# Partial sums of a seven-product block matmul: added up in one PSUM bank and copied by ScalarE, or added on VectorE

## The chip, the core and the metric

The kernel runs on one core of one Trainium2 chip. The metric is the device time of one execution in microseconds. The kernel before takes 2735.14 us (median of three runs, 2733.68 to 2735.2). A core has TensorE (PE in the profile), which multiplies matrices into the eight banks of PSUM; ScalarE (ACT) and VectorE (DVE), which read PSUM and work elementwise; GpSimd (POOL); and DMA queues, most of them issued by SyncE (SP). Each engine has its own list of instructions, and semaphores order the engines against each other.

## What is computed

Eight images of 3008 tokens and 256 channels in float32 go through a filter in the frequency domain, and then through a two-layer network with ELU between the layers:

```
X = rfft(x, axis=1);  y = irfft(X * (filt_r + 1j*filt_i), n=3008, axis=1)
x = y.reshape(8 * 3008, 256)
h = x @ w_in                                   # 256 -> 2048
g = where(h > 0, h, exp(min(h, 0)) - 1)        # ELU
return g @ w_out                               # 2048 -> 256
```

## The kernel before

The transforms are done by matmuls with small tables (units `a_unit`, `b_unit`, `bi_unit`, `n_unit`). The two layers are done in **items**: one item is one image `b` (8), one block `m` of 512 tokens (6 per image; block 0 has 448) and one quarter `q` (4) of the 2048 hidden channels, 192 items in all. Both layers see their matrices as 2 by 2 blocks and use seven block products in place of eight; sums of blocks are made before and after. An item has seven products of the first layer ("up", U1 to U7) and, one item later, seven of the second ("down", D1 to D7). Every product is two matmuls of 128 by 128 by 256 in float32, which the profile shows as four MATMUL records.

The products of the first layer go to banks of the pool `psM`, four banks used in turn; the second layer's sums stay in four banks `po0` to `po3` over the four quarters.

```python
    psM = pool("psM", 4, space=PSUM)
...
        def mm(n, key, start):                 # product n of the first layer into bank `key`
            if start:
                banks[key] = psM.tile([P, 2, 256], FP32, tag="mx", name="ph" + key)
            for a in range(2):
                nc.tensor.matmul(banks[key][:, a, 0:h], w_in[q][:, COMBO[n], a, :], y[n],
                                 start=start and a == 0, stop=True, skip_group_check=True)   # L310
            return banks[key][:, :, 0:h]
        def add(o, i0, i1):                                                                  # L315
            nc.vector.tensor_tensor(out=g[o], in0=i0, in1=i1, op=ALU.add)
        def elu_exp(n, src):                   # exp(-relu(-h)), two operations on ScalarE
            e = es[n] = ep.tile([P, 2, 256], FP32, tag="e", name="e")[:, :, 0:h]
            nc.scalar.activation(out=e, in_=src, func=AXT.Relu, scale=-1.0)                  # L321
            nc.scalar.activation(out=e, in_=e, func=AXT.Exp, scale=-1.0)                     # L322
        def elu_max(n, src):                   # max(e - 1, h) on VectorE
            nc.vector.scalar_tensor_tensor(out=g[n], in0=es[n], scalar=1.0, in1=src, ...)    # L326

        def s1(): nc.scalar.activation(out=g["t1"], in_=mm(1, "a", True), func=AXT.Copy)     # L330
        def s6(): add("t2", mm(6, "b", True), g["t1"])
        def s2(): p = mm(2, "a", False); elu_exp("b11", p); elu_max("b11", p)
        def s5(): add("t4", mm(5, "c", True), g["t2"])
        def s7(): add("b22", mm(7, "d", True), g["t4"]); elu_exp("b22", g["b22"])
        def s3(): add("b12", mm(3, "c", False), g["t2"]); elu_max("b22", g["b22"])
        def s4(): elu_exp("b12", g["b12"]); add("b21", mm(4, "d", False), g["t2"])
        def tail():
            elu_exp("b21", g["b21"]); elu_max("b12", g["b12"])
            # t1 = b12 - b11; b12 = b22 - b12; elu_max b21; t2 = b22 - t1; t4 = b21 - t2    (L359 to L363)
```

(The one-line bodies are printed here in place of several lines each.) The tail's four subtractions make the block sums that the second layer's products take. In the last quarter, q = 3, the second layer's four banks are put together into the output block `c`, on VectorE after the item's own tail:

```python
        def step(n):                           # product n of the second layer
            ...matmuls into po...                                                            # L383
            if q == 3 and n in (5, 7):
                t = k[i] = kp.tile([P, 2, 256], FP32, tag="k%d" % i, name="k%d" % i)
                nc.scalar.activation(out=t[:, :, 0:h], in_=po[i][:, :, 0:h], func=AXT.Copy)  # L387
                if n == 7:
                    p3 = t[:, 0, 0:h]
                    nc.vector.tensor_tensor(out=p3, in0=p3, in1=k[0][:, 1, 0:h], op=ALU.add) # L390
        def tail():                            # q == 3 alone: six adds of 128x256
            add(c12, po[2][:, 1, 0:h], p1); add(c11, po[2][:, 0, 0:h], p1); add(p7, p7, c12) # L401
            add(c12, c12, p35); add(c21, po[3][:, 0, 0:h], p7); add(c22, p7, p5)
```

The main loop writes the steps of item `i` and of item `i-1` in a fixed order, with units of the transforms at two places, in the middle and at the end:

```python
            for k in "UDUDUDUUD":              # U1 D1 U6 D3 U2 D5 U5 U7 D7
                ...
            for fn, a in plan.get((i, 0), ()): # a_unit, n_unit, o_unit (output transposes)
                fn(*a)
            for k in "UDUDD":                  # U3 D6 U4 D2 D4
                ...
            up_tail(); down_tail()
            for fn, a in plan.get((i, 1), ()): # bi_unit, b_unit, n_unit
                fn(*a)
```

The units at the places repeat with every image, that is, every 24 items. By the place of an item in its image: `a_unit` in the middle of items 0, 2, 3, 4, 6, 7; `o_unit`, two transposes on VectorE, in the middle of items 1, 5, 9, 13, 17, 21; `n_unit` in the middle of items 8, 12, 16, 20 and at the end of 1 and 5; `b_unit` at the end of items 9 to 16 and `bi_unit` at the end of 11 to 18. A `b_unit` has four multiplications of 128x512 on VectorE that read its two banks.

Of the kernel before, what the change touches and what calls it, by code (L numbers as in the profile page):

```python
# [10 lines left out]
FP32 = mybir.dt.float32  # L11
U32 = mybir.dt.uint32
AXT = mybir.ActivationFunctionType
# [82 lines left out]
def kernel(  # L96
# [15 lines left out]
    def pool(name, bufs, **kw):  # L112
        return ctx.enter_context(tc.tile_pool(name=name, bufs=bufs, **kw))
# [13 lines left out]
    yd = pool("yd", 2, space=DRAM)  # L127
    fdp = pool("fdp", 1, space=DRAM)
    psO = pool("psO", 1, space=PSUM)
    psM = pool("psM", 4, space=PSUM)  # L130

    gb, gr, gi = (glob.tile([P, 2, 64], FP32, name=n) for n in ("gb", "gr", "gi"))

# [7 lines left out]

    def raw(src, row, ap, col=0):
        return bass.AP(tensor=src.tensor, offset=src.offset + row * D + col, ap=ap)

# [12 lines left out]
    def a_unit(b, c):  # L159
        t = t1s[b, c] = t1p.tile([P, XC, D], FP32, tag="t1", name="t1")  # L160
        xt, w = xs.pop((b, c)), tas.pop((b, c))
        for r in (0, 2):
            ps = psM.tile([P, 2, D], FP32, tag="mx", name="psa")
            for u in range(2):
                nc.tensor.matmul(ps[:, u, :], w[:, r + u, :], xt[:, r + u, :], start=True, stop=True)  # L165
            nc.scalar.activation(out=t[:, r:r + 2, :], in_=ps, func=AXT.Copy)

# [41 lines left out]
    def b_unit(b, g, f=None):  # L211
        t = t2s.pop((b, g))
        f = fbufs[(b * NG + g) % FBUFS] if f is None else f
        re, im = (psM.tile([P, 2, D], FP32, tag="mx", name=n) for n in ("psr", "psi"))
        for o, a in ((0, 0), (64, 2)):
            for ps, k in ((re, LO), (im, HI)):
                tile_mm(ps[o:o + 64], gb, k, t[:, a:a + 2, :], g == 0 and a == 0)
        sr, si = (sp.tile([P, 2, D], FP32, tag=n, name=n) for n in ("sr", "si"))
        p, q = (qp.tile([P, 2, D], FP32, tag=n, name=n) for n in ("sp", "sq"))

        nc.vector.tensor_tensor(out=sr, in0=re, in1=f[:, 0], op=ALU.mult)
        nc.vector.tensor_tensor(out=si, in0=re, in1=f[:, 1], op=ALU.mult)  # L222
        nc.vector.tensor_tensor(out=p, in0=im, in1=f[:, 1], op=ALU.mult)  # L223
        nc.vector.tensor_tensor(out=q, in0=im, in1=f[:, 0], op=ALU.mult)
        nc.gpsimd.tensor_tensor(out=sr, in0=sr, in1=p, op=ALU.subtract)  # L225
        nc.gpsimd.tensor_tensor(out=si, in0=si, in1=q, op=ALU.add)
        ss[b, g] = (sr, si)

    def bi_unit(b, g):
        s = ss.pop((b, g))  # L230
        t = t3s[b, g] = t3p.tile([P, 4, D], FP32, tag="t3", name="t3")
        pa, pb = (psM.tile([P, 2, D], FP32, tag="mx", name=n) for n in ("pva", "pvb"))
        for o, table, sv in ((0, gr, s[0]), (64, gi, s[1])):
            for ps, k in ((pa, LO), (pb, HI)):
                tile_mm(ps[o:o + 64], table, k, sv, g == 0 and k == LO)
        nc.scalar.activation(out=t[:, 0:2, :], in_=pa, func=AXT.Copy)  # L236
        nc.scalar.activation(out=t[:, 2:4, :], in_=pb, func=AXT.Copy)

    def y_write(b, g):
        if g == 0:  # L240
# [16 lines left out]
    def n_unit(b, m):  # L257
        t, w, h = t4s.pop((b, m)), tns.pop((b, m)), half(m)
        rows = []
        for dh in range(2):  # L260
            y = yp.tile([P, 512], FP32, tag="y%d" % dh, name="y%d" % dh)
            ps = psM.tile([P, 512], FP32, tag="mx", name="psn")
            for q, i in enumerate(order(m)):
                nc.tensor.matmul(ps[:, ts(q, P)], t[:, i - 4 * m, ds(dh * P, P)], w[:, i - 4 * m, :],  # L264
                                 start=True, stop=True)
            nc.scalar.activation(out=y[:, 0:2 * h], in_=ps[:, 0:2 * h], func=AXT.Copy)
            rows += [y[:, 0:h], y[:, h:2 * h]]
        s = yp.tile([P, 3, 256], FP32, tag="ys", name="ys")
        ys[b, m] = combine(*rows, *(s[:, i, 0:h] for i in range(3)))
# [20 lines left out]
        return {1: b11, 2: b21, 3: b22, 4: t4, 5: t1, 6: t2, 7: b12}  # L290

    G_TAGS = (("g1", ("b11", "b12")), ("g2", ("b21", "b22")), ("g3", ("t1", "t2")), ("g4", ("t4",)))
    UPS = (1, 6, 2, 5, 7, 3, 4)
    DOWNS = (1, 3, 5, 7, 6, 2, 4)

    def up_steps(b, m, q):

        h = half(m)
        y = ys[b, m]
        g = {}  # L300
        for tag, names in G_TAGS:
            t = gp.tile([P, len(names), 2, 256], FP32, tag=tag, name=tag)
            g.update({n: t[:, i, :, 0:h] for i, n in enumerate(names)})
        banks = {}

        def mm(n, key, start):
            if start:
                banks[key] = psM.tile([P, 2, 256], FP32, tag="mx", name="ph" + key)
            for a in range(2):
                nc.tensor.matmul(banks[key][:, a, 0:h], w_in[q][:, COMBO[n], a, :], y[n],  # L310
                                 start=start and a == 0, stop=True, skip_group_check=True)
            return banks[key][:, :, 0:h]

        def add(o, i0, i1):
            nc.vector.tensor_tensor(out=g[o], in0=i0, in1=i1, op=ALU.add)  # L315

        es = {}

        def elu_exp(n, src):
# [4 lines that stand above are left out]
        def elu_max(n, src):  # L324

            nc.vector.scalar_tensor_tensor(out=g[n], in0=es[n], scalar=1.0, in1=src, op0=ALU.subtract, op1=ALU.max)  # L326


        def s1():
            nc.scalar.activation(out=g["t1"], in_=mm(1, "a", True), func=AXT.Copy)  # L330

        def s6():
            add("t2", mm(6, "b", True), g["t1"])

        def s2():
            p = mm(2, "a", False)
            elu_exp("b11", p)
            elu_max("b11", p)

        def s5():  # L340
            add("t4", mm(5, "c", True), g["t2"])

        def s7():
            add("b22", mm(7, "d", True), g["t4"])
            elu_exp("b22", g["b22"])

        def s3():
            add("b12", mm(3, "c", False), g["t2"])
            elu_max("b22", g["b22"])

        def s4():
            elu_exp("b12", g["b12"])
            add("b21", mm(4, "d", False), g["t2"])

        def tail():
            elu_exp("b21", g["b21"])
            elu_max("b12", g["b12"])
            t1, b12, b22 = g["t1"], g["b12"], g["b22"]
            nc.vector.tensor_tensor(out=t1, in0=b12, in1=g["b11"], op=ALU.subtract)  # L359
            nc.vector.tensor_tensor(out=b12, in0=b22, in1=b12, op=ALU.subtract)  # L360
            elu_max("b21", g["b21"])
            nc.vector.tensor_tensor(out=g["t2"], in0=b22, in1=t1, op=ALU.subtract)
            nc.vector.tensor_tensor(out=g["t4"], in0=g["b21"], in1=g["t2"], op=ALU.subtract)  # L363
            g_of[b, m, q] = {1: g["b11"], 2: g["b21"], 3: b22, 4: g["t4"], 5: t1, 6: g["t2"], 7: b12}

        return (s1, s6, s2, s5, s7, s3, s4), tail


    PLACE = {1: (0, 0), 5: (0, 1), 3: (1, 0), 7: (1, 1), 2: (2, 0), 6: (2, 1), 4: (3, 0)}

    def down_steps(b, m, q):
# [7 lines left out]
        def step(n):  # L379
            i, u = PLACE[n]  # L380
            for a in range(2):

                nc.tensor.matmul(po[i][:, u, 0:h], w_out[q][:, COMBO[n], a, :], g[n][:, a, :],  # L383
                                 start=q == 0 and a == 0 and n in (1, 3, 6, 4), stop=True, skip_group_check=True)
            if q == 3 and n in (5, 7):
                t = k[i] = kp.tile([P, 2, 256], FP32, tag="k%d" % i, name="k%d" % i)
                nc.scalar.activation(out=t[:, :, 0:h], in_=po[i][:, :, 0:h], func=AXT.Copy)  # L387
                if n == 7:
                    p3 = t[:, 0, 0:h]
                    nc.vector.tensor_tensor(out=p3, in0=p3, in1=k[0][:, 1, 0:h], op=ALU.add)  # L390

        def tail():
            if q != 3:
# [6 lines left out]
            def add(o, i0, i1):  # L400
                nc.vector.tensor_tensor(out=o, in0=i0, in1=i1, op=ALU.add)  # L401

            add(c12, po[2][:, 1, 0:h], p1)
            add(c11, po[2][:, 0, 0:h], p1)
            add(p7, p7, c12)
# [110 lines left out]
    with tc.manual_schedule():  # L516
# [109 lines left out]
        for i in range(-PER, len(items) + 2):  # L626
            ups, up_tail = up_steps(*items[i]) if 0 <= i < len(items) else ((), None)
            downs, down_tail = down_steps(*items[i - 1]) if 1 <= i <= len(items) else ((), None)
            ups, downs = list(ups), list(downs)
            for k in "UDUDUDUUD":  # L630
                s = ups if k == "U" else downs
                if s:
                    s.pop(0)()
            for fn, a in plan.get((i, 0), ()):
                fn(*a)
            for k in "UDUDD":
                s = ups if k == "U" else downs
                if s:
                    s.pop(0)()
# [38 lines left out]
```

## Time and profile before

| | before |
|---|---|
| time, median of three | 2735.14 us |
| span of the profiled run | 2733.4 us |
| MATMUL records of the two layers (L310, L383) | 10752 |
| granted TensorE clock, mean | 0.978 |
| HBM traffic | 79 GB/s over the span |
| down products (L383), busy | 1325.1 us |
| ScalarE relu and exp (L321, L322), busy | 948.0 us |
| VectorE adds on products (L315), busy | 647.3 us |

The profile gives each engine's busy time, and groups of instructions by source line and tile. Matmuls are pipelined and their ends are modelled, so two MATMUL records on one engine overlap; the distance from one start to the next says more than the duration. The granted clock is that of TensorE; it was at half for several stretches of the first 219 us and for the last 11 us, and full between.

### The profile page before, as it was taken

Reading aid. Unit: us, or ns where it says so; the run is one execution under the profiler, and the core shown is the slowest. Engines: PE = TensorE matmul, PEld = TensorE weight load, DVE = VectorE, ACT = ScalarE, POOL = GpSimd, SP = SyncE. Lnnn points to the kernel's source line nnn. Section 1 sums busy time; section 2 is a strip of 40 time slices with the busy share of each in tenths; the row PEclk is TensorE's granted clock in tenths of the full one; section 3 lists DMA queues with packets and bytes.
Section 4 is the critical chain, followed back from the end, with each engine's and each line's share of the span. In section 5 each row is a group of like instructions: output and inputs, shape, how many; then the busy total and the mean of one; then the engine's idle time right before and its main releaser. Section 6 shows DMA issues by size and latency. Waiting matters only on the chain.

```text
span 2733.4 us, 36388 instructions
## 1 busy us (share of the span) xinstructions
PE 2626.5 (96%) x12992; PEld 2237.5 (82%) x12992; DVE 2066.9 (76%) x3531; ACT 1286.0 (47%) x2177; POOL 275.6 (10%) x325
## 2 busy tenths in 40 slices
PE   2689999999999999999999999999999999999998
PEld 1278778987899878998789877898789987898887
DVE  3877877778777777768876787777877777777876
ACT  2244454544545444454444445454454544444443
POOL 4311210002000120001200021000210012000000
PEclk7599999999999999999999999999999999999999
DMA  9645321434114331242323333143421323110100
GB/s 244 180 116 122 88 69 37 110 96 102 43 42 121 78 93 37 74 120 68 79 50 88 88 85 73 37 110 97 98 57 41 79 62 95 37 39 19 26 22 16
DMA packets 229428, 214.47 MB, mean 78 GB/s; under 512 B 131620, under 2 KB 192566, under 8 KB 229248
## 3 DMA queue, kind: packets, MB, share of 16 engines
q1 hardware_dynamic: 210592, 173.65, 25.8%
q0 software_dynamic: 17792, 36.93, 5.6%
q8 instruction: 103, 1.69, 0.3%
q10 hardware_dynamic: 864, 1.57, 0.2%
q14 instruction: 77, 0.63, 0.1%
HBM read 136.97 MB, written 78.12 MB: 79 GB/s over the span
## 4 chain that ended last, share of the span: by engine, by line
PE 77%; DVE 12%; ACT 5%; DMA 2%; issue 2%; POOL 0%; DVEq 0%; SPq 0%; ACTq 0%; POOLq 0%
PE po L383 34%; PE pha L310 11%; PE phc L310 10%; PE phd L310 10%; PE phb L310 5%; DVE g L315 3%; PE psa L165 3%; ACT e L322 2%; ACT e L321 2%; PE pva L209 2%; PE psn L264 2%; PE psr L209 2%; DVE c L401 2%; DVE g L326 1%; DVE g L359 1%
## 5 line engine op out<-in xcount | busy, mean ns | idle before, releaser
L383 PE MATMUL po<-g,wo 128*128 128x256 f32 (+1 forms) x5376 | 1325.1, 375 | 0.0
L383 PEld LDWEIGHTS po<-g,wo 128*128 128x128 f32 x5376 | 1022.0, 190 | 116.4
L321 ACT ACTIVATE e<-g 128x512 f32<-128x512 f32 (+1 forms) x576 | 357.6, 621 | 616.2 <-DVE g L315 616.2
L322 ACT ACTIVATE e<-e 128x512 f32<-128x512 f32 (+1 forms) x768 | 477.5, 622 | 24.3
L310 PE MATMUL pha<-y,wi 128*128 128x256 f32 (+1 forms) x1536 | 396.2, 380 | 9.3 <-ACT g L330 9.2
L326 DVE SCALAR_TENSOR_TENSOR g<-e,g 128x512 f32<-128x512 f32 (+1 forms) x576 | 387.0, 672 | 12.9 <-ACT e L322 12.8
L315 DVE TENSOR_TENSOR g<-phc,g 128x512 f32<-128x512 f32 (+1 forms) x384 | 257.7, 671 | 141.3 <-PE phc L310 141.3
L321 ACT ACTIVATE e<-pha 128x512 f32<-128x512 f32 (+1 forms) x192 | 112.9, 588 | 532.5 <-PE pha L310 532.5
L310 PEld LDWEIGHTS pha<-y,wi 128*128 128x128 f32 x1536 | 285.3, 190 | 93.3 <-ACT t L236 34.1
L326 DVE SCALAR_TENSOR_TENSOR g<-e,pha 128x512 f32<-128x512 f32 (+1 forms) x192 | 129.4, 674 | 253.8 <-ACT e L322 253.8
L315 DVE TENSOR_TENSOR g<-phd,g 128x512 f32<-128x512 f32 (+1 forms) x384 | 260.6, 679 | 70.1 <-PE phd L310 50.0
L225 POOL TENSOR_TENSOR sr<-sr,sp 128x512 f32<-128x512 f32 x64 | 81.0, 1265 | 1289.4 <-DVE sp L223 1289.4
L310 PE MATMUL phc<-y,wi 128*128 128x256 f32 (+1 forms) x768 | 196.3, 378 | 5.0 <-DVE g L315 5.0
L310 PE MATMUL phc<-ys,wi 128*128 128x256 f32 (+1 forms) x768 | 195.3, 377 | 2.6 <-DVE si L222 2.6
L310 PE MATMUL phd<-y,wi 128*128 128x256 f32 (+1 forms) x768 | 194.7, 376 | 1.3
L310 PE MATMUL phd<-ys,wi 128*128 128x256 f32 (+1 forms) x768 | 194.2, 375 | 0.0
L310 PE MATMUL phb<-ys,wi 128*128 128x256 f32 (+1 forms) x768 | 193.8, 375 | 0.4 <-DVE ys L288 0.4
L310 PEld LDWEIGHTS phc<-y,wi 128*128 128x128 f32 x768 | 140.6, 190 | 29.5 <-DVE g L315 13.3
L310 PEld LDWEIGHTS phc<-ys,wi 128*128 128x128 f32 x768 | 145.3, 191 | 23.7 <-issue 7.8
L310 PEld LDWEIGHTS phd<-y,wi 128*128 128x128 f32 x768 | 144.7, 190 | 22.4 <-PE phc L310 6.5
L330 ACT ACTIVATE g<-pha 128x512 f32<-128x512 f32 (+1 forms) x192 | 112.7, 587 | 103.9 <-PE pha L310 103.7
L310 PEld LDWEIGHTS phd<-ys,wi 128*128 128x128 f32 x768 | 146.4, 191 | 16.7
(105 smaller groups left out, 2706.3 us busy)
## 6 DMA issues: line engine op xcount, KB each, us to landing
z<-t SPq DMA_DIRECT2D x192, 128.0 KB, 4.1
t<-z SPq DMA_DIRECT2D x128, 192.0 KB, 3.7
yd<-t SPq DMA_DIRECT2D x128, 192.0 KB, 2.8
t<-yd SPq DMA_DIRECT2D x192, 128.0 KB, 3.9
xc<-in_x_dram SPq DMA_DIRECT2D x84, 256.0 KB, 4.7
f<-fd POOLq DMA_DIRECT2D x112, 192.0 KB, 3.8
out_dram<-o SPq DMA_DIRECT2D x640, 32.0 KB, 1.6
tn<-tn_t SPq DMA_DIRECT2D x48, 256.0 KB, 3.8
```

The lines of the kernel that those rows point to most:

```text
L165: nc.tensor.matmul(ps[:, u, :], w[:, r + u, :], xt[:, r + u, :], start=True, stop=True)
L209: nc.tensor.matmul(ps[:, u:u + w, :], table[k, v, :], rhs[k, u:u + w, :], start=True, stop=True)
L225: nc.gpsimd.tensor_tensor(out=sr, in0=sr, in1=p, op=ALU.subtract)
L264: nc.tensor.matmul(ps[:, ts(q, P)], t[:, i - 4 * m, ds(dh * P, P)], w[:, i - 4 * m, :], start=True, stop=True)
L310: nc.tensor.matmul(banks[key][:, a, 0:h], w_in[q][:, COMBO[n], a, :], y[n], start=start and a == 0, stop=True, skip_group_check=True)
L315: nc.vector.tensor_tensor(out=g[o], in0=i0, in1=i1, op=ALU.add)
L321: nc.scalar.activation(out=e, in_=src, func=AXT.Relu, scale=-1.0)
L322: nc.scalar.activation(out=e, in_=e, func=AXT.Exp, scale=-1.0)
L326: nc.vector.scalar_tensor_tensor(out=g[n], in0=es[n], scalar=1.0, in1=src, op0=ALU.subtract, op1=ALU.max)
L330: nc.scalar.activation(out=g["t1"], in_=mm(1, "a", True), func=AXT.Copy)
L383: nc.tensor.matmul(po[i][:, u, 0:h], w_out[q][:, COMBO[n], a, :], g[n][:, a, :], start=q == 0 and a == 0 and n in (1, 3, 6, 4), stop=True, ...
L401: nc.vector.tensor_tensor(out=o, in0=i0, in1=i1, op=ALU.add)
```

## The change

In the first layer, products 1, 6, 5 and 3 now add up one after the other in one PSUM bank, "s". After each of the first three ScalarE copies the sum so far to SBUF (t1, t2, t4); after the fourth, b12 is read from the bank itself. Before, t2, t4 and b12 were made by adds on VectorE, and b11 was left in PSUM; now b11 is made by an add on VectorE. So per item two VectorE adds become ScalarE copies. The purpose is to take work from VectorE. Banks are now handed out by a list in the program, since "s" is held from U1 to U3 while others come and go. The order of the steps is changed to go with this. In the second layer's last quarter the two copies of `po0` and `po1` stand together after D7, and the add of L390 moves into the tail, which has seven adds instead of six. The number of matmuls is the same.

```diff
-    psM = pool("psM", 4, space=PSUM)
+    psM = pool("psM", 1, space=PSUM)
...
+    banks = [0, 1, 2, 3]
+    def bank(name, shape=(P, 2, D)):
+        i = banks.pop(0)
+        return i, psM.tile(list(shape), FP32, tag="m%d" % i, name=name)
...  (a_unit, b_unit, bi_unit, n_unit: take a bank from the list, give it back after the last reader)
-    UPS = (1, 6, 2, 5, 7, 3, 4)
+    UPS = (1, 2, 6, 5, 7, 3, 4)
...
         def s1():
-            nc.scalar.activation(out=g["t1"], in_=mm(1, "a", True), func=AXT.Copy)
+            keep("t1", mm(1, "s", True))
+        def s2():
+            add("b11", mm(2, "a", True), g["t1"])
+            done("a")
         def s6():
-            add("t2", mm(6, "b", True), g["t1"])
-        def s2():
-            p = mm(2, "a", False)
-            elu_exp("b11", p)
-            elu_max("b11", p)
+            keep("t2", mm(6, "s", False))
+            elu_exp("b11", g["b11"])
+            elu_max("b11", g["b11"])
         def s5():
-            add("t4", mm(5, "c", True), g["t2"])
+            keep("t4", mm(5, "s", False))
         def s7():
             add("b22", mm(7, "d", True), g["t4"])
-            elu_exp("b22", g["b22"])
         def s3():
-            add("b12", mm(3, "c", False), g["t2"])
+            p = mm(3, "s", False)
+            elu_exp("b12", p)
+            elu_exp("b22", g["b22"])
+            elu_max("b12", p)
+            done("s")
+        def s4():
+            add("b21", mm(4, "d", False), g["t2"])
+            done("d")
             elu_max("b22", g["b22"])
-        def s4():
-            elu_exp("b12", g["b12"])
-            add("b21", mm(4, "d", False), g["t2"])
         def tail():
             elu_exp("b21", g["b21"])
-            elu_max("b12", g["b12"])
...
-            if q == 3 and n in (5, 7):      (copy of one bank after D5, of the other after D7, add of L390)
+            if q == 3 and n == 7:
+                for i in range(2):
+                    t = k[i] = kp.tile([P, 2, 256], FP32, tag="k%d" % i, name="k%d" % i)
+                    nc.scalar.activation(out=t[:, :, 0:h], in_=po[i][:, :, 0:h], func=AXT.Copy)
...
+            add(p35, p35, p5)               (first of the tail's adds)
...
-            for k in "UDUDUDUUD":           (U1 D1 U6 D3 U2 D5 U5 U7 D7, units, U3 D6 U4 D2 D4)
+            for k in "UUDUDDU":             (U1 U2 D1 U6 D3 D5 U5, units, D7 U7 U3 D6 U4 D2 D4)
...
-            for k in "UDUDD":
+            for k in "DUUDUDD":
```

(`keep` is a ScalarE copy to SBUF; `done` puts a bank back on the list.)

More of the change, by code (lines that the diff above doesn't have):

```diff
@@ L162, in a_unit @@
         for r in (0, 2):
-            ps = psM.tile([P, 2, D], FP32, tag="mx", name="psa")
+            k, ps = bank("psa")
             for u in range(2):
@@ L166, in a_unit @@
             nc.scalar.activation(out=t[:, r:r + 2, :], in_=ps, func=AXT.Copy)
+            banks.append(k)
     def z_write(b, c):
@@ L213, in b_unit @@
         f = fbufs[(b * NG + g) % FBUFS] if f is None else f
-        re, im = (psM.tile([P, 2, D], FP32, tag="mx", name=n) for n in ("psr", "psi"))
+        (i0, re), (i1, im) = (bank(n) for n in ("psr", "psi"))
         for o, a in ((0, 0), (64, 2)):
@@ L224, in b_unit @@
         nc.vector.tensor_tensor(out=q, in0=im, in1=f[:, 0], op=ALU.mult)
+        banks.extend((i0, i1))
         nc.gpsimd.tensor_tensor(out=sr, in0=sr, in1=p, op=ALU.subtract)
@@ L231, in bi_unit @@
         t = t3s[b, g] = t3p.tile([P, 4, D], FP32, tag="t3", name="t3")
-        pa, pb = (psM.tile([P, 2, D], FP32, tag="mx", name=n) for n in ("pva", "pvb"))
+        (i0, pa), (i1, pb) = (bank(n) for n in ("pva", "pvb"))
         for o, table, sv in ((0, gr, s[0]), (64, gi, s[1])):
@@ L237, in bi_unit @@
         nc.scalar.activation(out=t[:, 2:4, :], in_=pb, func=AXT.Copy)
+        banks.extend((i0, i1))
     def y_write(b, g):
@@ L261, in n_unit @@
             y = yp.tile([P, 512], FP32, tag="y%d" % dh, name="y%d" % dh)
-            ps = psM.tile([P, 512], FP32, tag="mx", name="psn")
+            k, ps = bank("psn", (P, 512))
             for q, i in enumerate(order(m)):
@@ L266, in n_unit @@
             nc.scalar.activation(out=y[:, 0:2 * h], in_=ps[:, 0:2 * h], func=AXT.Copy)
+            banks.append(k)
             rows += [y[:, 0:h], y[:, h:2 * h]]
@@ L303, in up_steps, with done, keep @@
             g.update({n: t[:, i, :, 0:h] for i, n in enumerate(names)})
-        banks = {}
+        held = {}
         def mm(n, key, start):
             if start:
-                banks[key] = psM.tile([P, 2, 256], FP32, tag="mx", name="ph" + key)
+                held[key] = bank("ph" + key)
+            ps = held[key][1]
             for a in range(2):
-                nc.tensor.matmul(banks[key][:, a, 0:h], w_in[q][:, COMBO[n], a, :], y[n],
+                nc.tensor.matmul(ps[:, a, 0:h], w_in[q][:, COMBO[n], a, :], y[n],
                                  start=start and a == 0, stop=True, skip_group_check=True)
-            return banks[key][:, :, 0:h]
+            return ps[:, :, 0:h]
+        def done(key):
+            banks.append(held.pop(key)[0])
         def add(o, i0, i1):
             nc.vector.tensor_tensor(out=g[o], in0=i0, in1=i1, op=ALU.add)
+        def keep(o, i0):
+            nc.scalar.activation(out=g[o], in_=i0, func=AXT.Copy)
         es = {}
@@ L329, in s1, with s3 @@
         def s1():
-            nc.scalar.activation(out=g["t1"], in_=mm(1, "a", True), func=AXT.Copy)
+            keep("t1", mm(1, "s", True))
+        def s2():
+            add("b11", mm(2, "a", True), g["t1"])
+            done("a")
         def s6():
-            add("t2", mm(6, "b", True), g["t1"])
-        def s2():
-            p = mm(2, "a", False)
-            elu_exp("b11", p)
-            elu_max("b11", p)
+            keep("t2", mm(6, "s", False))
+            elu_exp("b11", g["b11"])
+            elu_max("b11", g["b11"])
         def s5():
-            add("t4", mm(5, "c", True), g["t2"])
+            keep("t4", mm(5, "s", False))
         def s7():
             add("b22", mm(7, "d", True), g["t4"])
+        def s3():
+            p = mm(3, "s", False)
+            elu_exp("b12", p)
             elu_exp("b22", g["b22"])
-        def s3():
-            add("b12", mm(3, "c", False), g["t2"])
+            elu_max("b12", p)
[3 more added lines that the diff above has]
+            done("d")
             elu_max("b22", g["b22"])
-        def s4():
-            elu_exp("b12", g["b12"])
-            add("b21", mm(4, "d", False), g["t2"])
         def tail():
             elu_exp("b21", g["b21"])
-            elu_max("b12", g["b12"])
             t1, b12, b22 = g["t1"], g["b12"], g["b22"]
@@ L364, in tail @@
             g_of[b, m, q] = {1: g["b11"], 2: g["b21"], 3: b22, 4: g["t4"], 5: t1, 6: g["t2"], 7: b12}
-        return (s1, s6, s2, s5, s7, s3, s4), tail
+        return (s1, s2, s6, s5, s7, s3, s4), tail
     PLACE = {1: (0, 0), 5: (0, 1), 3: (1, 0), 7: (1, 1), 2: (2, 0), 6: (2, 1), 4: (3, 0)}
@@ L384, in step @@
                                  start=q == 0 and a == 0 and n in (1, 3, 6, 4), stop=True, skip_group_check=True)
[L385 to L390, printed above, removed]
+            if q == 3 and n == 7:
+                for i in range(2):
+                    t = k[i] = kp.tile([P, 2, 256], FP32, tag="k%d" % i, name="k%d" % i)
+                    nc.scalar.activation(out=t[:, :, 0:h], in_=po[i][:, :, 0:h], func=AXT.Copy)
         def tail():
@@ L401, in add @@
                 nc.vector.tensor_tensor(out=o, in0=i0, in1=i1, op=ALU.add)
+            add(p35, p35, p5)
             add(c12, po[2][:, 1, 0:h], p1)
@@ L629 @@
             ups, downs = list(ups), list(downs)
-            for k in "UDUDUDUUD":
+            for k in "UUDUDDU":
                 s = ups if k == "U" else downs
```

## The prediction, made before the changed kernel ran

> **What bounds the kernel now.** First the page's busy times, then the table of a few windows, then the timeline of one item. The page:
>
> ```profile
> PE 2626.5 (96%) x12992; PEld 2237.5 (82%) x12992; DVE 2066.9 (76%) x3531; ACT 1286.0 (47%) x2177; POOL 275.6 (10%) x325
> ```
>
> PE at 96% could still hide small waits, so I looked at windows: a plain item (only the 14 products), then two items behind a q = 3 item, one without a unit at its end and one with (us, busy us and count of PE, PEld, DVE, ACT, POOL).
>
> ```profile
> 446.31:458.40 12.09, 12.09 (x57) 10.64 (x56) 8.80 (x15) 5.74 (x10) 0.00 (x0) 1.00 0.42 100
> 1238.50:1252.16 13.66, 13.48 (x70) 10.88 (x68) 13.13 (x24) 6.60 (x12) 0.00 (x0) 1.00 0.08 15
> 1295.60:1310.50 14.90, 14.62 (x76) 10.80 (x72) 14.50 (x27) 6.58 (x12) 3.50 (x4) 1.00 0.38 94
> ```
>
> In the plain item TensorE is full: 14 products in 12.09 us, one start each 0.863 us, no gap. There DVE (8.80) has room. Behind a q = 3 item DVE is nearly full too (13.13 of 13.66, 14.50 of 14.90). The timeline of the second window shows what that does, DVE first, then PE (start, us, what; idle before and who ended it):
>
> ```profile
> 1241.94 0.69 DVE L363 TENSOR_TENSOR g<-g,g 128x512 f32<-128x512 f32 x1
> 1242.55 0.75 DVE L401 TENSOR_TENSOR c<-po,k 128x256 f32<-128x256 f32 x2
> ...
> 1244.35 0.42 DVE L401 TENSOR_TENSOR c<-k,k 128x256 f32<-128x256 f32 x1
> 1244.68 0.68 DVE L315 TENSOR_TENSOR g<-phb,g 128x512 f32<-128x512 f32 x1
> 1245.28 0.68 DVE L326 SCALAR_TENSOR_TENSOR g<-e,pha 128x512 f32<-128x512 f32 x1
> 1245.87 0.68 DVE L315 TENSOR_TENSOR g<-phc,g 128x512 f32<-128x512 f32 x1
> ```
>
> ```profile
> 1245.41 1.03 PE L383 MATMUL po<-g,wo 128*128 128x256 f32 x4
> 1246.61 1.13 PE L310 MATMUL phc<-y,wi 128*128 128x256 f32 x4 [0.17 <-DVE g L315]
> ```
>
> The previous item's last subtraction starts 3.44 us after this item began (1238.50), then come the six adds of `c` (2.13 us), and only at 6.18 us the first add of this item. U3 accumulates into bank phc, which the add at 1245.87 to 1246.55 still reads; so U3 starts at 1246.61, 8.11 us in, not at 9 x 0.863 = 7.77. **The wait is 0.34 us**, and its products then take 0.967 instead of 0.863 us to the next, since their first weight load lies bare.
>
> Going through all PE starts of the trace, after 250 us only places 9, 13, 17 and 21 of an image's 24 items have such waits: about 0.35, 0.70, 0.70 and 0.15 us, 1.9 us an image, 15 us for eight images, some 17 with bare weight loads. In the first 225 us there are another 18 us, nearly all in items 1 (11 us, weight conversion) and 5 (4.3 us, memsets). The matmuls are untouched by the change, so **nothing below about 2735 - 17 - 18 = 2700 us can be had**, and 2% faster (2680) is out.
>
> [...] above, U3's wait delays D6 behind it, and this item's add stands behind six adds it has no need of. [...] the trace has 587 ns for copies from PSUM, 621 for relu or exp.
>
> **The change part by part.**
>
> *Work moved.* Per item DVE loses two adds of about 0.675 us (x192: 259 us off 2067), ACT gains two copies of 0.587 us (x192: 225 us onto 1286). Neither engine ends the time, so this pays only through waits of PE.
>
> *Waits removed.* The new DVE order has 11 operations per plain item, not 13, and no bank waits for an add from its queue except "a" and "d", which are used again late. I take all 17 us of steady waits off.
>
> *Waits added.* I wrote down both orders from the built programs. ACT now has: t1 copy, t2 copy, relu and exp of b11, **t4 copy**, [units, two `po` copies], relu and exp of b12, of b22, of b21. PE may start U6, U5, U3 only when t1, t2, t4 have been copied from the same bank. The relu of b11 waits for the add of b11 on DVE, which stands behind the previous item's tail; and the t4 copy stands behind that relu and exp. So a late DVE now reaches U3 through ACT. Rates from the timeline above and its neighbours: product end = start + 1.03; next engine 0.03 to 0.04 later; ACT 0.60 to 0.66 from start to start; DVE 0.60, or 0.72 behind a subtraction from SBUF.
>
> A plain item, from its start: U1 ends 1.03, t1 copied by 1.65; U6 needs it at 3 x 0.863 = 2.59. U6 ends 3.62, t2 copied by 4.25; U5 needs it at 5.18. U5 ends 6.21; U3 is due at 7.77, ends 8.80. ACT: relu b12 8.83, exp 9.46, to 10.09; relu b22 10.12, exp 10.78, to 11.41. DVE: max b12 10.12, add b21 10.72, max b22 11.45, subtractions 12.05 and 12.77, max b21 13.50, then 14.10 and 14.82, free about 15.5, which is 3.4 in the next item. There b11 is added 3.4 to 4.1, relu and exp end 5.6, before U5's end: the t4 copy ends 6.84 and **U3 has 0.9 us to spare**. The `b_unit`s add 2.4 us (four multiplications) on DVE against 2.06 us of PE, or against about 1.1 us where `b_unit` is alone (items 9, 10); that still fits.
>
> Behind a q = 3 item seven adds come first, 2.13 + 0.44 = 2.57 us: b11 is added at 6.0 to 6.65, relu 6.7, exp 7.35 to 7.98, t4 copied 8.0 to 8.6, U3 at 8.67. **Wait 0.9 us**, plus 0.10 for the bare weight load. These are places 1, 5, 9, 13, 17, 21, and none has an `a_unit` or `n_unit` in the middle that would push U3 back. By the same walk: place 9 and 21, 0.9 each; 13 and 17, behind a `bi_unit` and `b_unit`, 1.2 each; place 1, where the item has 224 columns and U3 is due at 9 x 0.756 = 6.8, 1.15; place 5, behind seven 224-column adds, 0.97. Sum 6.3, with weight loads 6.9 us an image, x8 = 55; less 2.3 for items 1 and 5 of the first image, counted below, and 0.6 in the last image, which has no `b_unit`: **+52 us**.
>
> *The beginning.* In item 1 the same ACT queue still stalls one product about 9 us, but the 2.2 us of smaller waits behind it should go; in item 5 memsets (2.7 us) come on top of the adds and I get 3.3 us for U3 against 4.3 now. Together -3.
>
> *The end.* The second copy of `po` and the add in the tail come 0.6 us later, but before D2's end, which the other adds wait for: 0.
>
> Sum: 2735 + 52 - 17 - 3 = 2767; I take **2766 us** (+1.1%).
>
> **Rivals.**
> 1. *Relief without a new wait*: the ACT copies get through in time, steady waits vanish, about 2715 us. For it: ACT is busy 47% and plain items have 0.9 us of slack on each of the three copies. Against: the six items per image, where the order on ACT is fixed and DVE is known to be 6 us late. I give it one in eight, with the halfway cases.
> 2. *A longer wait*: after the late U3 a second stall follows (b22's add behind the `o_unit`'s two transposes, then bank "d" or D3 of the next item), or the backlog carries over. I find the next item starting with DVE 3.4 us behind again, since max b12 hangs on U3 and not on the backlog. If wrong, waits of 1.6 us or more, 2790 us and above.
> 3. *ACT as the bound*: 11 activations of about 0.61 are 6.7 us of 12.1; no.
> 4. *DMA*: transfers are unchanged and hidden; no.
>
> **Range and chances.** My 48 waits of about 1.1 us may each be off by 0.3 us, 15 us in sum, to one side since they repeat exactly; the beginning by 5. With rival 1 below, the range is 2738 to 2785. Faster by 2% is excluded but for a gross error (0.01); slower by 2% needs 2790 (0.07).
>
> **What would show it.** The waits should list PE (phs) waiting for ACT's copies about 50 times, at places 1, 5, 9, 13, 17, 21, near 1 us; waits of phc for DVE gone. DVE near 1810 us, ACT near 1510. Plain items should stay at 12.09 us. In the timeline of a place-9 item the relu of b11 should start 6.7 us in, ended by the DVE add, with the t4 copy after its exp and U3 right behind. If plain items lengthen, my slack was wrong; if places 1 to 21 show no wait, the ACT step is wrong.

## The result, and the profile after

The changed kernel takes 2762.51 us (median of four runs, 2760.79 to 2764.03), the kernel before 2734.44 us beside it: a ratio of **1.0102 (95% interval 1.0085 to 1.012)**, 28 us slower. The prediction was 2766 us.

The page of the kernel after, busy us of each engine, share of the span, instructions:

```profile
PE 2646.8 (96%) x12992; PEld 2243.2 (81%) x12992; DVE 1811.9 (66%) x3147; ACT 1492.5 (54%) x2561; POOL 275.4 (10%) x325
```

The purpose was met: VectorE has 384 instructions and 255 us less, ScalarE 384 instructions and 207 us more. TensorE has the same matmuls and its share is the same 96%. Its busy time is 20 us longer, but this line does not show where or why. The windows do, for a plain item and for the items at places 9 and 13 (us, then busy us and count of PE, PEld, DVE, ACT, POOL):

```profile
451.91:464.00 12.09, 12.09 (x58) 10.67 (x57) 6.90 (x12) 6.43 (x11) 0.00 (x0) 1.00 0.43 96
924.33:938.28 13.95, 13.74 (x69) 10.82 (x67) 11.92 (x23) 7.21 (x12) 0.00 (x0) 1.00 0.11 19
981.71:996.93 15.22, 14.69 (x76) 10.93 (x72) 13.22 (x25) 7.66 (x14) 3.49 (x4) 1.00 0.39 98
```

The plain item still takes 12.09 us, now with 6.90 us of VectorE instead of 8.80. The items behind a q = 3 item became longer (13.66 to 13.95, 14.90 to 15.22) although VectorE does less in them. Whom TensorE waits for, after the first image (waits of PE between 400 and 2500 us: total, times, longest):

```profile
PE phs L323 <- ACT g L334: 12.3, 38, 0.5
PE phd L323 <- DVE g L331: 1.7, 10, 0.2
```

Products into "s" wait for the ScalarE copies (L334), and products into "d" for VectorE's add of b22 (L331). The waits of phc for VectorE that the kernel before had are gone. The list gives only the part of a wait in which the modelled end of the matmul before had passed, and leaves out short ones, such as that of U4 at place 9 below; the distances between starts, used below, are the full cost.

The timeline of the place-9 item, which starts at 924.33 us. VectorE:

```profile
926.82 0.69 DVE L385 TENSOR_TENSOR g<-g,g 128x512 f32<-128x512 f32 x1
927.43 0.42 DVE L421 TENSOR_TENSOR k<-k,k 128x256 f32<-128x256 f32 x1
...
929.55 0.41 DVE L421 TENSOR_TENSOR c<-k,k 128x256 f32<-128x256 f32 x1
929.88 0.68 DVE L331 TENSOR_TENSOR g<-pha,g 128x512 f32<-128x512 f32 x1
931.93 0.69 DVE L345 SCALAR_TENSOR_TENSOR g<-e,g 128x512 f32<-128x512 f32 x1 [1.36 <-ACT e L341]
932.53 1.30 DVE L442 STREAM_TRANSPOSE o<-c 128x512 f32<-128x512 f32 x2
933.76 0.65 DVE L331 TENSOR_TENSOR g<-phd,g 128x512 f32<-128x512 f32 x1
```

ScalarE:

```profile
927.98 0.60 ACT L334 ACTIVATE g<-phs 128x512 f32<-128x512 f32 x1 [1.99 <-PE phs L323]
930.60 0.63 ACT L340 ACTIVATE e<-g 128x512 f32<-128x512 f32 x1 [2.02 <-DVE g L331]
931.26 0.63 ACT L341 ACTIVATE e<-e 128x512 f32<-128x512 f32 x1
931.80 0.58 ACT L334 ACTIVATE g<-phs 128x512 f32<-128x512 f32 x1
```

TensorE:

```profile
931.24 1.03 PE L323 MATMUL phd<-y,wi 128*128 128x256 f32 x4
932.43 1.13 PE L323 MATMUL phs<-y,wi 128*128 128x256 f32 x4 [0.17 <-ACT g L334]
933.40 1.03 PE L405 MATMUL po<-g,wo 128*128 128x256 f32 x4
934.47 1.13 PE L323 MATMUL phd<-ys,wi 128*128 128x256 f32 x4
```

This is the chain. VectorE has the last item's subtraction and seven adds before it (to 929.9), so b11 is added at 5.55 us into the item. ScalarE stood idle for 2.02 us with the relu of b11 at its head, and the copy of t4, whose product had ended at about 6.2 us, comes third, at 7.47 to 8.05. U3 starts at 8.10 us instead of 7.77 (932.43). Then U4 starts 0.20 us later than its place behind U3: VectorE's add of b22, behind max b11 and two transposes, ends only at 934.41.

Item lengths from one U1 to the next, read from the starts of the products, in the third image, tell the whole loss:

| place in the image | before | after |
|---|---|---|
| 1 | 12.38 | 13.47 |
| 5 | 13.87 | 14.57 |
| 9 | 13.66 | 13.95 |
| 13 | 14.92 | 15.22 |
| 17 | 14.05 | 14.37 |
| 21 | 12.35 | 12.83 |
| sum of the six | 81.23 | 84.41 |

The 18 other places are unchanged to 0.02 us. The six are 3.18 us longer in this image. The second to the seventh image are each 3.2 to 3.3 us longer, the first 5.2 and the last 1.7, together 26 of the 27 us between the two spans.

### The profile page after: what moved, and what is told of

It reads as the page before. It is cut to its first block, busy times and chain, and to the rows that moved or that the text cites. A ratio compares the mean times of both kernels' runs of the same rounds, so it can differ in the third digit from the quotient of the medians.

```text
span 2760.2 us, 36001 instructions
## 1 busy us (share of the span) xinstructions
PE 2646.8 (96%) x12992; PEld 2243.2 (81%) x12992; DVE 1811.9 (66%) x3147; ACT 1492.5 (54%) x2561; POOL 275.4 (10%) x325
## 4 chain that ended last, share of the span: by engine, by line
PE 73%; DVE 16%; ACT 5%; DMA 2%; issue 2%; POOL 0%; DVEq 0%; SPq 0%; ACTq 0%; POOLq 0%
PE po L405 31%; PE phs L323 20%; PE phd L323 9%; PE pha L323 4%; PE psn L275 3%; DVE g L345 3%; PE psa L173 3%; DVE c L421 3%; DVE g L331 2%; ACT e L341 2%; ACT e L340 2%; PE pva L218 2%; PE psr L218 2%; DVE g L382 1%; DVE g L385 1%
## 5 line engine op out<-in xcount | busy, mean ns | idle before, releaser
L334 ACT ACTIVATE g<-phs 128x512 f32<-128x512 f32 (+1 forms) x576 | 337.8, 586 | 576.9 <-PE phs L323 575.2
L331 DVE TENSOR_TENSOR g<-phd,g 128x512 f32<-128x512 f32 (+1 forms) x384 | 258.0, 672 | 270.3 <-PE phd L323 267.5
L323 PE MATMUL phs<-y,wi 128*128 128x256 f32 (+1 forms) x1536 | 401.6, 384 | 18.2 <-ACT g L334 18.2
L323 PE MATMUL phs<-ys,wi 128*128 128x256 f32 (+1 forms) x1536 | 388.8, 376 | 11.2 <-ACT g L334 11.2
L323 PEld LDWEIGHTS phs<-y,wi 128*128 128x128 f32 x1536 | 282.2, 191 | 117.7 <-ACT g L334 37.0
L323 PEld LDWEIGHTS phs<-ys,wi 128*128 128x128 f32 x1536 | 292.6, 191 | 45.0 <-ACT g L334 12.3
L345 DVE SCALAR_TENSOR_TENSOR g<-e,phs 128x512 f32<-128x512 f32 (+1 forms) x192 | 130.0, 677 | 223.0 <-ACT e L341 223.0
L340 ACT ACTIVATE e<-phs 128x512 f32<-128x512 f32 (+1 forms) x192 | 112.9, 588 | 291.7 <-PE phs L323 291.6
L323 PE MATMUL pha<-y,wi 128*128 128x256 f32 (+1 forms) x768 | 193.9, 375 | 0.0
L323 PEld LDWEIGHTS pha<-y,wi 128*128 128x128 f32 x768 | 146.4, 191 | 16.4
L382 DVE TENSOR_TENSOR g<-g,g 128x512 f32<-128x512 f32 (+1 forms) x192 | 130.7, 681 | 6.7
L385 DVE TENSOR_TENSOR g<-g,g 128x512 f32<-128x512 f32 (+1 forms) x192 | 130.7, 681 | 6.6
```

The lines of the kernel that those rows point to most:

```text
L323: nc.tensor.matmul(ps[:, a, 0:h], w_in[q][:, COMBO[n], a, :], y[n], start=start and a == 0, stop=True, skip_group_check=True)
L334: nc.scalar.activation(out=g[o], in_=i0, func=AXT.Copy)
```

## The experiments

All were timed against the kernel before on the same chip, and read by the same table. The two edits to the order (the first two runs) were run alone and together. Three theories stood against each other. **A**: what is late is VectorE, behind a q = 3 item; the order on ScalarE only decides at which product that lateness reaches TensorE. **B**: the copy of t4 behind the relu is the whole loss. **C**: the two more copies, or adding four products in one bank, cost by themselves.

### The copy of t4 first

```diff
         def s6():
             keep("t2", mm(6, "s", False))
-            elu_exp("b11", g["b11"])
-            elu_max("b11", g["b11"])
         def s5():
             keep("t4", mm(5, "s", False))
+            elu_exp("b11", g["b11"])
+            elu_max("b11", g["b11"])
```

> The changed kernel with ELU's relu, exp and max of b11 written after the copy of t4 instead of before it; the o_unit stays. Theory A (the late VectorE sets the loss, ScalarE's order only decides at which product it lands): U3 no longer waits (0.33 to 0.66 us at six items an image, now zero), but max b11 comes at 8.2 us into the item instead of 7.6, the two transposes and the add of b22 behind it end at 10.65, and U4, due at 9.5, waits 1.2 us. Loss per place 1.3 us instead of 0.66 (9, 21), 1.06 (13, 17), 1.09 (1), 0.70 (5): about +2.6 us an image, 2783 us. Rival B (U3's wait for the t4 copy is the whole loss): the U3 waits go and nothing comes back, 2762 - 28 = 2734 us. Rival C (the loss is the two extra copies, or adding into one bank as such): 2762, no change.

Measured: 2774.91 us, ratio 1.0148 (1.0132 to 1.0163). It got slower still. The timeline of its place-9 item, starting at 926.64 us, VectorE and then TensorE:

```profile
934.69 0.69 DVE L345 SCALAR_TENSOR_TENSOR g<-e,g 128x512 f32<-128x512 f32 x1 [1.81 <-ACT e L341]
935.30 1.30 DVE L442 STREAM_TRANSPOSE o<-c 128x512 f32<-128x512 f32 x2
936.52 0.65 DVE L331 TENSOR_TENSOR g<-phd,g 128x512 f32<-128x512 f32 x1
```

```profile
934.41 1.03 PE L323 MATMUL phs<-y,wi 128*128 128x256 f32 x4
935.27 1.03 PE L405 MATMUL po<-g,wo 128*128 128x256 f32 x4
937.23 1.13 PE L323 MATMUL phd<-ys,wi 128*128 128x256 f32 x4 [0.93 <-DVE g L331]
```

U3 is on time (7.77 us in), so its wait is gone, as A and B both expect. But max b11 now starts at 8.05 us, the transposes and the add of b22 follow, and U4, due at 9.49, starts at 10.59: a wait of 1.1 us (expected 1.2). The six places sum to 86.19 us, 1.8 us an image more than after (expected 2.6). B falls; the loss only moved. C, "no change", does not fit either.

### The transposes at the end of their item

```diff
-                at(t + PER + 4 * m + 5, 0, o_unit, b, m)
+                at(t + PER + 4 * m + 5, 1, o_unit, b, m)
```

> The changed kernel with the o_unit (two transposes, 1.25 us of VectorE) moved from the middle of its item to the item's end, the order of ScalarE untouched. Theory A: U3's waits stay at 0.33 to 0.66 us, U4's waits (0.20 to 0.33 us) go, about -1.7 us an image; but item 10, which follows an o_unit and a b_unit that is alone, now starts with VectorE 5.9 us late and gets a U3 wait of about 0.6 us: net -1 us an image, 2754 us. Rival B (only U3's wait counts): 2762 or, by the new wait, a little more. Rival C: 2762.

Measured: 2749.78 us, ratio 1.0055 (1.004 to 1.007). U3 and U4 of its place-9 item, which starts at 922.25 us:

```profile
930.35 1.13 PE L323 MATMUL phs<-y,wi 128*128 128x256 f32 x4 [0.17 <-ACT g L334]
932.18 1.03 PE L323 MATMUL phd<-ys,wi 128*128 128x256 f32 x4
```

U3 is as late as after (8.10 us in), and U4 follows two products behind it without a wait of its own. So the U4 waits are gone (place 9: 13.65, place 13: 14.91), and the U3 waits stand as they were (phs for ScalarE, 29.4 us in 51 waits, the same as after). Place 10 has a new loss, 13.64 us instead of 13.30: a wait of 0.23 us and the bare weight load's 0.10, where a wait of 0.6 was expected. Net 1.5 us an image gained, 12.7 us in all, for 8 expected. As A has it.

### Both edits

> The changed kernel with both edits: relu, exp and max of b11 after the t4 copy, and the o_unit at the item's end. Theory A: U3 finds t4 copied at 6.85 us (due 7.77), the add of b22 ends at 9.45, just as U4 is due at 9.5; nearly all steady waits go, 5.2 us an image or 41 us, and the beginning gets a few us shorter: 2717 us, faster than both kernels. Rival B: the same as the first run of this call. Rival C: 2762.

("The first run" there is the one with the copy of t4 first.) Measured: 2720.75 us, ratio **0.9946 (0.9929 to 0.9962)**: 42 us less than after, where the two edits alone gave +12 and -13. All waits of TensorE for ScalarE's copies or VectorE's adds on first-layer products that the list still has in this run:

```profile
PE phs L323 <- ACT g L334: 11.2, 3, 9.4
...
PE phd L323 <- DVE g L331: 2.5, 1, 2.5
```

Four waits, and the starts show them in items 0, 1, 2 and 5 of the first image. Of the later ones only a trace is left at place 1, where U4 starts 0.04 us late and its weight load adds 0.10. The six places have 12.52, 13.88, 13.22, 14.17, 13.31 and 12.10 us, 79.20 in sum: 2.0 less than before, 5.2 less than after, as expected. In the place-9 item, starting at 911.73 us, VectorE does max b11 and at once the add of b22; then U3 and U4 on TensorE:

```profile
919.78 0.69 DVE L345 SCALAR_TENSOR_TENSOR g<-e,g 128x512 f32<-128x512 f32 x1 [1.81 <-ACT e L341]
920.39 0.68 DVE L331 TENSOR_TENSOR g<-phd,g 128x512 f32<-128x512 f32 x1
```

```profile
919.50 1.03 PE L323 MATMUL phs<-y,wi 128*128 128x256 f32 x4
921.22 1.03 PE L323 MATMUL phd<-ys,wi 128*128 128x256 f32 x4
```

The add ends at 921.07, 9.34 us in, and U4 starts when it is due, at 9.49; U3 is on time too, at 7.77. This run makes the same copies, out of the same bank, as the changed kernel, and more than the whole loss is gone: C falls, and with it the new way of handing out banks as a cause, which this run keeps too.

### The seventh add undone

```diff
                 for i in range(2):
                     ...the two copies of po...
+                p3 = k[1][:, 0, 0:h]
+                nc.vector.tensor_tensor(out=p3, in0=p3, in1=k[0][:, 1, 0:h], op=ALU.add)
...
-            add(p35, p35, p5)
```

> The changed kernel with one part undone: the add of the two po copies stands again behind the copies after D7, so the q = 3 tail has six adds and not seven (0.44 us less ahead of b11's add). Theory A: everything behind it comes 0.44 us earlier, the U3 waits at places 9 and 21 go, those at 13, 17 and 1 shrink to 0.2, and U4 waits 0.2; about -2.5 us an image, 2742 us. Rival C (copies or bank as such): 2762, since no copy and no bank changes.

Measured: 2744.88 us, ratio 1.0032 (1.0019 to 1.0045), 18 us less than after; its five times spread from 2738.25 to 2746.4. U3 and U4 of the place-9 item, which starts at 920.46 us:

```profile
928.23 1.12 PE L323 MATMUL phs<-y,wi 128*128 128x256 f32 x4
930.26 1.13 PE L323 MATMUL phd<-ys,wi 128*128 128x256 f32 x4
```

U3 is on time (7.77 us in), as expected, and U4 waits 0.20 us; at 13 and 17 U3 still waits 0.31 us, where 0.2 was expected. At places 9, 13, 17, 21 and 1 the item is 0.34 or 0.35 us shorter (13.61, 14.88, 14.02, 12.49, 13.13), at 5 0.31 us: one add of 128x256 taken out from ahead of b11's add gives its start-to-start time of 0.33 us back at each place (at 5 it has 224 columns). I had taken 0.44 us. The six places give 2.0 us an image, 16 us in eight. So undoing this one move gives back 16 to 18 of the 28 us, and it is a side of the change that has nothing to do with the bank. How it would add to the two edits above was not run.

### The memsets of item 4 on GpSimd

```diff
-            at(4, 1, nc.vector.memset, f, 0.0)
+            at(4, 1, nc.gpsimd.memset, f, 0.0)
```

This is on top of both edits.

> The third run of the first call (t4 copied first, o_unit late) with the three one-off memsets of item 4 given to GpSimd instead of VectorE. Theory A: the 2.7 us by which U4 of item 5 in the first image still waits is VectorE being 2.7 us later there; it goes, nothing else moves: 2720.75 - 2.7 = 2718 us. Rival (that wait is DMA or weight conversion): 2721.

Measured: **2716.44 us, ratio 0.993 (0.9915 to 0.9944)**, the fastest version here, 19 us faster than the kernel before. ("The third run of the first call" is the run with both edits.) Item 5 of the first image takes 13.88 us instead of 16.67, 2.8 us less for 2.7 expected; the wait of phd is gone from the list. The time fell by 4.3 us. This run and the two controls below were made on another chip than the runs above (kernel before: 2735.89 us there, 2735.23 above), and of the rest 1.8 us lies ahead of item 2, where the edit changes nothing.

### Controls on the kernel before

The `o_unit` at the end of its item, in the kernel before:

> The kernel before with the o_unit at its item's end. Theory A: in the old order the waits at places 9, 13, 17 and 21 come ahead of the transposes on VectorE, so they stay, and the later items have room: 2735 us, no change. Rival D (what the third run of the first call gained is the o_unit's move alone, whatever the order): about 2735 - 13 = 2722 us.

("The third run" there is again the run with both edits.) Measured: 2735.03 us, ratio 0.9997 (0.9988 to 1.0005). Every item of the image keeps its length to 0.03 us. The move pays only where something that TensorE needs stands behind the transposes, so D falls.

VectorE's max of b11 behind the add of t4, in the kernel before:

```diff
         def s2():
             p = mm(2, "a", False)
             elu_exp("b11", p)
-            elu_max("b11", p)
+            es["p"] = p
         def s5():
             add("t4", mm(5, "c", True), g["t2"])
+            elu_max("b11", es["p"])
```

> The kernel before with VectorE's max of b11 written after the add of t4, the same kind of edit as moving the t4 copy ahead. Theory A: U3's waits at places 9 (0.36) and 21 (0.25) go; at 13 and 17 U5 and U7 still wait for the banks that the b_unit's multiplications read (0.7 us): about -0.75 us an image, 2729 us. So the old kernel keeps some 10 us of waits that the new one with the same kind of edit has not. Rival D' (moving work in the queue gives the old kernel as much as the new one): about 2718 us.

Measured: 2734.37 us, ratio 0.9997 (0.9989 to 1.0006): nothing, where I expected 6 us. Places 9 and 21 gave 0.16 and 0.17 us, where I had taken 0.36 and 0.25; places 13 and 17 lost 0.20 and 0.22 us, where U5's wait for its bank grew from 0.35 to 0.55 us. VectorE is nearly full in those items (14.50 of 14.90 us at place 13 of the kernel before, the prediction's third window), and what is put ahead for one product is late for another. That the old division of work can't be ordered better is not shown by one try.

## Why the prediction was right, point by point

- **TensorE bounds, plain items stay.** Right: 12.09 us in both, and 96% in both. VectorE, foretold near 1810 us, has 1811.9; ScalarE, foretold near 1510, has 1492.5.
- **The chain.** Right in every link: VectorE's tail, the add of b11, its relu at ScalarE's head, the t4 copy behind its exp, U3. It showed at exactly the six places named, 1, 5, 9, 13, 17, 21. What it costs that the copy of t4 stands behind the relu in ScalarE's list shows best at place 13, in the product of t4 and then ScalarE's relu, exp and copy:

```profile
987.00 1.03 PE L323 MATMUL phs<-ys,wi 128*128 128x256 f32 x4
988.41 0.63 ACT L340 ACTIVATE e<-g 128x512 f32<-128x512 f32 x1 [2.34 <-DVE g L331]
989.07 0.63 ACT L341 ACTIVATE e<-e 128x512 f32<-128x512 f32 x1
989.61 0.58 ACT L334 ACTIVATE g<-phs 128x512 f32<-128x512 f32 x1
```

The product ended at 988.03, yet ScalarE stayed idle until 988.41 and copied t4 only at 989.61, as third. At place 9 the product ended (930.54) just before the relu started (930.60), so there the cost is the relu and exp ahead of the copy, and not idleness.
- **The size of the U3 wait.** Too large: 1.0 us foretold at place 9 with the bare weight load, 0.43 measured. b11's add began at 5.55 us and not at 6.0: the seventh add costs 0.33, and the last subtraction came 0.24 us sooner than in my walk. And I had put 0.66 us from the start of an exp to the copy behind it; it is 0.54: the copy, which takes nothing from the exp, starts 0.09 us before its end (931.26 + 0.63 = 931.89, next start 931.80). From the relu to the exp, which takes its result, it is 0.66: the exp starts 0.03 us after the relu's end (930.60 + 0.63 = 931.23, next start 931.26). The error of 0.57 us is twice the 0.3 us that the range allowed for one wait.
- **No second stall.** Wrong: U4 waits for the add of b22, 0.20 us at place 9 and 0.33 at place 1, and its weight load lies bare once more (0.96 us from U4's start to the next product's, not 0.863). I had this under the rivals and gave it only to the case of 2790 us. It is small after the late U3, but the first experiment shows that it is the firmer limit: with U3 on time it is 1.1 us, of which 0.45 us come from that edit itself, which moves max b11 from 7.60 to 8.05 us into the item.
- **The beginning.** Wrong in sign: -3 foretold, +4.2 measured up to item 6, 2.3 of it in item 5. There the U3 wait is 3.58 us, for 3.3 foretold; but the products behind it then ran at half clock, which cost 3.0 us more. I had read the like stretches of the kernel before as waits: 1.8 us of item 5's 4.3, and the 2.2 us of "smaller waits" in item 1. Those were products at half clock, 1.3 to 1.7 us apart instead of 0.757, behind the long stall:

```profile
153.20:157.50 4.30, 4.30 (x12) 3.90 (x13) 3.32 (x7) 1.12 (x2) 0.00 (x0) 0.50 0.00 0
```

They did not go: item 1 took 23.64 us before and 24.31 after. The other 1.9 us lie in items 0 and 1 and ahead of them, where two traces of the same steps differ as much: the kernel before with a late `o_unit`, which has the steps of the kernel before up to item 5, reached item 6 at 220.52 us, the kernel before at 222.76.
- **The sum.** Steady part: +35 foretold (52 - 17), +23 measured; beginning: 7 us the other way. The 2766 is near 2762.5 because the two errors had opposite signs, and the steady part hides two more such errors: by the starts in the third image the U3 waits with their weight loads are 3.6 us an image, where 6.9 were foretold, and those of U4, foretold as none, 1.8. The 17 us of old waits taken off were about right: with both edits an image takes 2.0 us less than before, 16 us in eight. So the chain, the places and the sign were understood; that the number came this close was luck.
- **Two readings of the trace.** The 587 and 621 ns are means over items of 448 and 512 columns; at 512 alone they are 596 and 630, and these count. And the item at 1238.50 us does have a unit at its end, a `b_unit`; what sets it apart from the one at 1295.60 is that no unit stands at the end of the item before it.

## What to carry to other kernels

When a result is copied out of an accumulating bank so that the next product may add to it, the copy becomes a gate of the matmul engine, and it must not stand in its engine's list behind anything that can be late for other reasons. Look for the few items in which the helper engine has extra work, not at plain ones or at shares of busy time: the change freed 255 us of VectorE and lost 28 us, and with two edits to the order of its steps it gained 14 instead. And try the edits together: the lateness moved from one product to the next, so that one edit alone made it worse and the two brought 42 us.

## What the runs showed of the hardware that I had not expected

The stall of TensorE in item 5 of the first image cost twice. In the kernel after, the granted clock is at half for 6.8 us (216.93 to 223.76 us) from the last 0.95 us of the 3.58 us stall in item 5 on, and the products behind the stall are 1.71 us apart and not 0.863. U7, U3 and D6 around the stall, then the table of windows of the kernel after: up to the stall's first part, over its end, and behind it (the column behind POOL is the granted clock):

```profile
213.43 1.03 PE L323 MATMUL phd<-y,wi 128*128 128x256 f32 x4
217.88 2.07 PE L323 MATMUL phs<-y,wi 128*128 128x256 f32 x4 [3.42 <-ACT g L334]
219.74 1.91 PE L405 MATMUL po<-g,wo 128*128 128x256 f32 x4
```

```profile
206.50:215.50 9.00, 7.96 (x37) 6.69 (x36) 8.41 (x17) 2.16 (x4) 5.81 (x6) 1.00 0.80 190
215.50:219.00 3.50, 1.12 (x3) 0.94 (x4) 2.14 (x4) 1.74 (x3) 3.10 (x4) 0.70 0.59 153
219.00:224.00 5.00, 5.00 (x14) 3.98 (x13) 2.01 (x4) 2.38 (x4) 0.00 (x0) 0.52 0.47 72
```

In the kernel before, the stall in item 5 is 2.53 us (U3 starts at 214.86, due at 212.33), and the clock is at half from 215.54 to 218.95 us, 3.4 us. In the run with both edits a stall of 2.70 us by the starts in item 5, of U4, came with no half clock: the two windows of that run, from 208 us to behind the stall, have a granted clock of 1.00:

```profile
208.00:217.50 9.50, 9.50 (x45) 8.20 (x44) 8.91 (x17) 2.76 (x5) 8.45 (x7) 1.00 0.68 172
217.50:224.70 7.20, 4.67 (x30) 4.17 (x29) 5.18 (x10) 5.49 (x9) 1.83 (x4) 1.00 0.60 115
```

So in these three runs the length of the stall alone does not decide: 2.53 us had half clock behind it and 2.70 us had not. What decides was not shown.
